# Block-local attention and a squared-gate feed-forward in one kernel: the work from the third unit on in another written order, and pairs of weight pieces in one tile

## The chip, the cores and the metric

The kernel runs on one core of a Trainium2 chip. The metric is the time of the device in microseconds (us), the median of several executions. A profile is taken of one execution; its times count from the first instruction. The engines are named PE (TensorE, matrix products; PEld its weight loads), DVE (VectorE), ACT (ScalarE), POOL (GpSimd) and SP (SyncE, which here only issues DMA transfers). Each engine runs its instructions in the order in which they are written.

## What is computed

Batch 4, 8 heads, 768 positions, 64 columns a head; 3072 tokens of 512 columns go into a feed-forward of 2048 columns.

```python
k_sum = k.reshape(B, H, nb, 32, D).max(axis=3)      # summaries of blocks of 32 keys
v_sum = v.reshape(B, H, nb, 32, D).mean(axis=3)
scores_l = scale * q @ k^T                          # kept where |i - j| < 16
scores_s = scale * q @ k_sum^T + log(32)
a = softmax(concat([scores_l_masked, scores_s]))
x = a @ concat([v, v_sum])                          # heads side by side: 3072 x 512
h = x @ w_in
g = where(h >= 1, h, where(h <= -1, 0, (h + 1)^2 / 4))
out = g @ w_out
```

## The kernel before

The 3072 tokens are cut into seven **units** (0 to 6) of 384, 384, 256 and four times 512 tokens; the first three are the *classic* units. Heads go in four pairs. The feed-forward is cut into 16 blocks f of 128 columns. Each fp32 operand of the feed-forward is split into a rounded high part and a remainder, and a product takes three matmuls (high x low, low x high, high x high).

Units 0 to 2 multiply x by w_in directly (L573). Units 3 to 6 use a scheme with seven products (L598) instead of eight: sums and differences of w_in blocks are prepared once, while units 1 and 2 run, and kept in DRAM (`sets`), eight sets of 14 x 256 columns; in each later unit every set is loaded again in four pieces into a **ring** of rooms, those that held the pieces win 7 to 14 of w_in. The seven x operands lie in the rooms of win 0 to 6.

The weights come in as pieces: 16 of w_in and 16 of w_out, taken two at a time as 16 pairs: (win 0, win 1), then (wout i-1, win i+1), at last (wout 14, wout 15). Each piece is [128, 2, 512] floats and has a room of its own in `wpool`, with a tag such as `win7`. The room takes first some of the first unit's inputs (`FIRST`), then the raw 64-bit words, then the two halves (high and remainder).

The order of all work is written out by hand as two texts, `OPENING` and `REST`. A word is a step: its first sign names a function, the others are hexadecimal numbers (unit, then pair of heads or block or set, then part). Each engine's queue, SP's and POOL's DMA issues too, follows these texts. After `OPENING` two pools are closed, and others are opened in their place: `att_later` (with two rooms of the tag merged), `ps_acc` (4) and `ps_att` (2). The steps that matter here:

| step | what it does | engine, line |
|---|---|---|
| r, k, q, y, v | load raw keys, windowed keys, queries, raw values, windowed values of unit and pair | SP, L294, L305, L321, L326, L339 |
| R, C | maxima of key blocks; their copy behind the windowed keys | DVE L354, POOL L359 |
| s, n, i, g, h, l, t, p | scores; mask; maxima; exponentials; reciprocals; scaling; 12 turns of blocks; values | PE L512, DVE L519, L526, ACT L530, DVE L534, POOL L540, DVE L552, PE L561 |
| u, z, x, X | sums of values, turned, spread; result of attention | DVE, POOL, ACT or DVE |
| F, G, H, I, J, O | product with w_in (unit, block, quarter); gate in three steps; its high part; its remainder | PE L573, ACT L663, L667, DVE L671, ACT L676, POOL L681 |
| B, ( | product with w_out, for all row tiles or for one | PE L694 |
| U, o | result out of the accumulator; its store | ACT L705 or DVE L703, SP L709 |
| %, & | prepare a set; store it in `sets` | POOL, DVE, ACT; SP |
| ^, <, > | differences, high part and remainder of x operands | POOL L486, ACT L494, POOL L498 |
| {cqn | load piece n of set q for unit c into the ring | POOL L585 |
| 1cqn, 9 | product n of set q; its sums | PE L598; DVE L611, ACT L607 |
| a, b, c, d, e | weights: scaling of the top words, low words, joining, high part, remainder | ACT L242, L248, DVE L255, L260, POOL or ACT L267, POOL L272 |

Rooms that are shared: k and v of units 2 and later, the converted words of the weights and, before, the first unit's results are tiles of tag w (3 rooms); r and y of units 2 and later, and v of unit 1, are tiles of tag v (2 rooms); results of unit 1 and later and the tiles of % are tiles of tag merged (2 rooms).

Of the kernel before, what the change touches and what calls it, by code (L numbers as in the profile page):

```python
# [42 lines left out]
CLASSIC = 3  # L43
WIDTH = [sum(n for _, _, n in unit) * QB for unit in BLOCKS]
# [29 lines left out]
F140 F141 t208 v20 t200 F142 &03 y21 t209 %017 H13 I13 t20a J12 O12 x200 t207 t20b F143 t204 t202 F150 t206 J13 t205  # L74
t201 r22 &05 u21 F151 p20 G14 F152 H14 q21 X20 I14 %100 C210 %101 %111 O13 F153 L20 %102 F160 s21 F161 %103 R22 G15
n211 n210 %110 i21 H15 I15 z21 g212 g210 k22 y22 v21 %104 %112 C220 g213 g211 F162 %113 h21 B12 F170 F171 x210 %114
u22 l210 l211 t21b t213 t210 &20 F172 F173 F163 J14 B13 q22 O14 t216 t21a t214 t219 B14 &21 &04 G16 t217 J15 t211 H16
I16 O15 G17 &02 F180 t212 t215 %105 y23 r23 %106 F181 t218 q23 H17 p21 X21 F182 z22 %115 I17 J16 %107 F183 F190 O16
L21 %116 s22 G18 u23 n220 &13 n221 i22 H18 I18 g220 g222 g223 g221 R23 F191 %117 x220 h22 F192 %200 %201 %202 F193 k23
# [15 lines left out]
H27 I27 R41 %612 F290 &62 F291 &63 g320 g325 J27 g321 g326 g322 %613 g324 g323 g327 O26 O27 F292 F293 %614 u40 %615
G29 h32 C330 %701 F283 %700 B26 H29 G28 H28 %702 I29 %703 I28 %704 B27 l320 F2b0 F2b1 %705 J29 J28 %616 l321 F2b2 q33
r42 F2b3 F2a0 F2a1 &30 %706 O28 G2b %617 t325 t323 t32a O29 &65 k40 &70 t320 H2b t326 I2b t321 t329 t32b t328 t327
%707 F2a2 F2a3 B28 J2b G2a H2a <30 O2b {300 F2d0 t324 t322 F2d1 F2d2 F2d3 I2a G2d B29 %711 H2d {303 J2a s33 O2a >30
{302 %710 n330 n331 i33 I2d F2c0 F2c1 F2c2 F2c3 G2c H2c y42 I2c B2a F2f0 v33 F2e0 F2f1 F2e1 F2f2 g335 g331 J2c &71
g336 g330 g333 {311 ^30 %712 F2f3 F2e2 F2e3 B2b {312 g334 &01 g337 %713 g332 %714 R42 h33 O2c C400 G2f u42 l330 l331  # L100
<33 H2f J2d O2d x330 p32 >33 I2f %715 1300 B2c &64 y43 X32 B2d t330 t338 9300 %716 t33b t339 {313 J2f t33a t336 t334
t332 y41 G2e {301 {310 O2f %717 t337 t335 t331 t333 1303 H2e p33 I2e J2e X33 <31 O2e <36 ^31 ^32 s40 <32 B2e u41 n401
n400 B2f i40 <34 >31 g405 g402 g400 >32 1301 9303 1302 k41 &73 >34 G300 g404 g401 g407 ^33 g406 g403 U21 H300 9301
1304 >36 z41 9304 <35 9302 1310 9305 1311 9310 1306 G311 H311 z40 h40 I300 9307 >35 G301 H301 I311 l400 l401 9313 r43
v40 1305 9306 1312 I301 9311 G310 1313 x400 H310 1316 t405 I310 J30 t40b t401 t400 t406 1314 J31 O31 O30 {321 t407 q42
(312 {322 {320 t403 t402 (311 {323 v41 &75 t409 C410 U20 {330 t40a t408 t404 (310 (302 q41 G320 H320 (313 9312 I320
9314 p40 9317 X40 G321 z42 9315 (301 H321 s41 I321 G331 n411 n410 i41 (303 1320 H331 J32 1315 9316 9320 1322 (300 O32
{331 g410 I331 9321 R43 G330 1323 g416 H330 1324 I330 9324 9322 g413 g411 J33 {343 O33 9325 1321 u43 1326 1325 9326
(331 g417 g412 (332 (321 k42 g415 g414 h41 {341 G351 H351 (333 (322 y50 v42 l410 q43 (330 9323 l411 G350 G340 {340
9327 I351 {333 H340 I340 H350 I350 t41b J35 G341 t418 t411 t417 t412 {342 (323 (320 1330 t415 t414 9330 t41a C420 O35  # L110
{332 &72 x410 1331 (350 y52 &74 1332 t419 t413 t410 t416 H341 9331 9333 I341 (351 p41 G360 H360 k50 X41 (353 1340 I360
J34 9340 O34 u50 s42 1342 1333 n420 1334 k43 q50 n421 i42 1335 9332 9334 g425 (343 g421 9335 g420 {351 9336 G371 (341
9341 G370 g424 (352 H370 1344 H371 g426 I370 1336 g427 I371 1343 x420 J37 1341 9342 9337 {350 1345 g423 g422 9344 (342
G361 9345 h42 O37 H361 I361 G391 9346 H391 1346 l421 l420 9343 (340 (372 I391 G390 9347 H390 J36 (370 (373 C430 O36
1350 {353 I390 G380 {363 {352 {361 t420 t424 t42b t42a t423 C500 t422 H380 G381 9350 t428 t429 t421 t425 (363 t427
(362 (371 (361 1352 {360 H381 I380 t426 s43 v43 9351 I381 (360 1353 n431 n430 J39 1355 J38 1354 O39 i43 g436 9354 9352
# [699 lines left out]
```

## Time and profile before

| | |
|---|---|
| runs | 661.37, 664.34, 665.67 us; median 664.34 |
| profiled execution | 661.37 us, its span 659.6 us |
| busy share of the span | PE 94%, PEld 82%, DVE 71%, POOL 65%, ACT 57% |
| mean granted clock of TensorE | 0.977 |
| moved by DMA | 137.27 MB, 208 GB/s over the span |

Busy time of PE is modelled, since matmuls overlap. A row of the timeline has start, duration, engine, line, operation, tiles, count, and in brackets the idle time before it and what ended it. A row of waits has the engine and its instruction, what it waited for, then the total in us, how often, and the longest. A row of a stretch has the busy time of PE, PEld, DVE, ACT and POOL with the number of instructions, the granted clock, the share of the DMA engines and GB/s. A group of instructions has its count, busy us and mean ns of one, and the idle time before it.

### The profile page before, as it was taken

How to read it: one execution, taken by the hardware profiler on the slowest of the kernel's cores; microseconds unless marked ns; L12 is line 12 of the kernel's file. 1: busy time of each engine (PE TensorE's matmuls, PEld its weight loads, DVE VectorE, ACT ScalarE, POOL GpSimd, SP SyncE). 2: the span in 40 equal slices, each digit the busy share in tenths (PEclk: the TensorE clock that was granted, in tenths of full speed). 3: DMA queues.
4: the chain of work that ended last, by engine and by line, in shares of the span. 5: the costliest groups of instructions: out<-in, count | busy, mean ns of one | idle time of the engine just before them, and what ended most of it. 6: DMA issues, size and time to landing. Idle time of an engine off the chain costs nothing.

```text
span 659.6 us, 13521 instructions
## 1 busy us (share of the span) xinstructions
PE 618.7 (94%) x4772; PEld 538.7 (82%) x4772; DVE 466.3 (71%) x1081; ACT 375.8 (57%) x1042; POOL 428.2 (65%) x515
## 2 busy tenths in 40 slices
PE   7789999799999998899989999999989999889896
PEld 7678888678888877778978888888878988779795
DVE  4988786389888899888877978876767774433332
ACT  1789997354645575654557556438445456443343
POOL 1569999555778589855668845579736569542421
PEclk8989999989999999899999999999989999998999
DMA  8969930286776769679699787875668465670631
GB/s 296 309 211 368 299 124 17 95 261 207 221 239 176 230 203 358 155 231 326 204 248 279 203 260 211 258 219 166 177 202 261 133 198 158 188 228 14 209 117 64
DMA packets 90009, 137.27 MB, mean 208 GB/s; under 512 B 27862, under 2 KB 57686, under 8 KB 89942
## 3 DMA queue, kind: packets, MB, share of 16 engines
q1 hardware_dynamic: 71510, 77.68, 39.1%
q0 software_dynamic: 18432, 58.73, 29.0%
q8 instruction: 38, 0.62, 0.4%
q14 instruction: 29, 0.24, 0.1%
HBM read 115.41 MB, written 20.97 MB: 207 GB/s over the span
## 4 chain that ended last, share of the span: by engine, by line
PE 63%; DVE 11%; DMA 11%; ACT 6%; POOL 4%; issue 4%; SPq 0%; DVEq 0%; ACTq 0%; POOLq 0%
PE acc L694 30%; PE h L598 20%; PE h L573 6%; DMA ring<-sets 3%; DVE merged L623 3%; DMA kraw<-in_kT 3%; DMA out<-o 3%; PE s_ps L512 2%; PE o_ps L561 2%; DMA k<-in_kwin 2%; DVE t L671 1%; DVE turned_blocks L552 1%; ACT e L423 1%; POOL glo L681 1%; DMA vraw<-in_vT 1%
## 5 line engine op out<-in xcount | busy, mean ns | idle before, releaser
L694 PE MATMUL acc<-halveswout,ghi 128*128 128x512 f32 x768 | 239.7, 393 | 0.0
L681 POOL TENSOR_TENSOR glo<-t,ghi 128x512 fp32r<-128x512 f32 (+2 forms) x112 | 126.8, 1135 | 115.1 <-ACT ghi L676 102.4
L598 PEld LDWEIGHTS h<-xop,ring 128*128 128x128 f32 x1344 | 176.7, 192 | 25.7 <-DVE t L671 6.5
L598 PE MATMUL h<-xop,ring 128*128 128x256 f32 x1344 | 184.1, 286 | 11.8 <-DMA ring<-sets 4.8
L694 PEld LDWEIGHTS acc<-halveswout,ghi 128*128 128x128 f32 x768 | 145.6, 190 | 25.8
L694 PE MATMUL acc<-halveswout,glo 128*128 128x512 f32 x384 | 154.1, 401 | 2.7 <-ACT o L705 1.7
L663 ACT ACTIVATE t<-h,ones_half 128x256 f32<-128x256 f32 (+1 forms) x176 | 84.2, 489 | 100.7 <-DVE h L611 76.7
L573 PE MATMUL h<-x,halveswin 128*128 128x384 f32 (+1 forms) x576 | 104.8, 329 | 4.7 <-DVE t L671 3.0
L676 ACT CAST ghi<-t 128x512 fp32r<-128x512 f32 (+2 forms) x112 | 62.0, 557 | 72.5 <-PE acc L694 38.3
L552 DVE STREAM_TRANSPOSE turned_blocks<-e 32x256 f32<-32x256 f32 (+1 forms) x240 | 98.3, 409 | 7.0 <-POOL e L540 3.1
L573 PEld LDWEIGHTS h<-x,halveswin 128*128 128x128 f32 x576 | 91.9, 191 | 13.5 <-DVE t L671 5.1
L671 DVE SCALAR_TENSOR_TENSOR t<-h,t 128x256 f32<-128x256 f32 (+1 forms) x176 | 75.2, 442 | 39.1 <-ACT t L667 35.7
L585 POOL DMA_DIRECT2D ring<-sets x128 | 70.7, 558 | 36.0 <-PE h L598 31.0
L694 PEld LDWEIGHTS acc<-halveswout,glo 128*128 128x128 f32 x384 | 73.0, 190 | 16.0 <-ACT o L705 2.1
L667 ACT ACTIVATE t<-t 128x256 f32<-128x256 f32 (+1 forms) x176 | 73.6, 434 | 3.2
L611 DVE TENSOR_TENSOR h<-h,sums_so_far 128x256 f32<-128x256 f32 x128 | 52.2, 427 | 31.9 <-PE h L598 31.1
L611 DVE TENSOR_TENSOR sums_so_far<-h,sums_so_far 128x256 f32<-128x256 f32 x96 | 39.7, 420 | 41.3 <-PE h L598 38.2
L530 ACT ACTIVATE e<-e,den 128x120 f32<-128x120 f32 x144 | 55.1, 384 | 19.1 <-DVE den L526 18.9
L540 POOL TENSOR_TENSOR e<-e,den 128x480 f32<-128x480 f32 (+1 forms) x40 | 35.7, 912 | 20.6 <-DVE den L535 18.7
L623 DVE TENSOR_TENSOR merged<-merged 128x128 f32<-128x128 f32 x64 | 33.2, 528 | 7.0 <-POOL merged L620 5.6
L498 POOL TENSOR_TENSOR xop<-xraw,xop 128x512 fp32r<-128x512 f32 x28 | 36.1, 1300 | 1.8 <-ACT xop L494 1.6
L519 DVE SCALAR_TENSOR_TENSOR e<-s_ps,mask_sb 128x480 f32<-128x480 f32 (+1 forms) x40 | 22.6, 601 | 9.8 <-PE s_ps L512 9.8
(105 smaller groups left out, 660.3 us busy)
## 6 DMA issues: line engine op xcount, KB each, us to landing
ring<-sets POOLq DMA_DIRECT2D x96, 512.0 KB, 5.6
rawwin<-in_w_in SPq DMA_DIRECT2D x16, 512.0 KB, 10.5
rawwout<-in_w_out SPq DMA_DIRECT2D x16, 512.0 KB, 9.7
ring<-sets POOLq DMA_DIRECT2D x32, 256.0 KB, 4.7
out<-o SPq DMA_DIRECT2D x24, 256.0 KB, 5.3
k<-in_kwin SPq DMA_DIRECT2D x12, 480.0 KB, 5.1
v<-in_vwin SPq DMA_DIRECT2D x18, 288.0 KB, 5.7
kraw<-in_kT SPq DMA_DIRECT2D x13, 384.0 KB, 4.7
```

The source lines that it names most:

```text
L530: nc.scalar.activation(out=e, in_=e, func=AF.Exp, bias=dens[c, p][:, 0, u:u + 1], scale=1.0, accum_out=dens[c, p][:, 1, u:u + 1])
L552: nc.vector.transpose(out=turned_blocks[kb * SB:(kb + 1) * SB, :2 * nt, qb * SB:(qb + 1) * SB], in_=e[qb * SB:(qb + 1) * SB, :, at:at + SB])
L573: nc.tensor.matmul(hs[c, f][:, :w], weight["win", f][:, part, k * P:(k + 1) * P], x, start=(k == 0 and n == 0), stop=(k == NK - 1 and n == 2))
L585: nc.gpsimd.dma_start(out=flat, in_=cols)
L598: nc.tensor.matmul(hs[c, q, n][:, :HALF], weights[:, wp, kk], x[:, xp, kk], start=(kk == 0 and m == 0), stop=(kk == 1 and m == 2))
L611: nc.vector.tensor_tensor(out=of if to is None else so_far[:, to], in0=of, in1=so_far[:, so], op=ALU.add)
L663: nc.scalar.activation(out=t, in_=h, func=AF.Relu, bias=ones_half, scale=0.5)
L667: nc.scalar.square(out=t, in_=t)
L671: nc.vector.scalar_tensor_tensor(out=t, in0=h, scalar=1.0, in1=t, op0=ALU.max, op1=ALU.min)
L676: nc.scalar.copy(out=hi, in_=ts[c, f])
L681: nc.gpsimd.tensor_tensor(out=lo, in0=ts[c, f], in1=hi.bitcast(F32), op=ALU.subtract)
L694: nc.tensor.matmul(acc[c, i], a[:, rows], weight["wout", f][:, part], start=(f == first and n == 0), stop=(f == last and n == 2))
```

## The change

1. `REST` is another order of the same 2700 steps and, new in it, the six steps that ended `OPENING` (U00, U01, U02, o02, o01, o00). `OPENING` is otherwise the same.
2. Pairs: both pieces of a pair lie in one tile [128, 2, 2, 512] of tag `w0` to `w15`; pair 14 (`APART`) keeps two tiles, since win 15's room later holds `sums_so_far`. For the 15 others, the scaling of the top words (a), the high part (d) and the remainder (e) are one instruction over 1024 columns where there were two over 512.
3. The x operands and the ring are slices of the pairs' tiles where they were tiles of their own in the same rooms.
4. Of the first unit's results, 0 and 1 now lie in rooms of tag merged; only 2 lies in tag w.

The end of `OPENING` and the beginnings of `REST`:

```diff
-J10 I11 F120 J11 O10 U00 F121 F122 U01 O11 F123 U02 o02 o01 o00
+J10 I11 F120 J11 O10 F121 F122 O11 F123
 REST
-%000 r20 k20 %001 q20 %002 %010 %011 %003 %004 %012 R20 %013 %005 %006 C200 %014 s20 n200 n201 &40 r21 k21 i20 g200
-y20 F130 F131 %015 g203 g201 g202 v22 R21 u20 h20 %007 G12 &00 F132 z20 F133 H12 l201 B10 I12 %016 G13 B11 l200 t203
+k20 F130 U00 r21 q20 r20 U01 R21 R20 C200 G12 U02 H12 F131 F132 F133 s20 I12 G13 H13 n201 n200 o01 %000 %001 o00 i20
+%002 y20 %003 I13 %011 %010 F150 B10 F151 F152 F140 %004 F141 F142 g200 g202 g203 g201 %012 %005 %006 h20 l200 l201
+B11 %013 u20 %014 J12 %007 k21 C210 t201 t205 %015 t202 q21 v20 o02 &31 &60 O12 y21 &40 F153 F143 z20 J13 G14 x200 O13
```

Of the last unit, the ring loads of its sets 2 to 6 with the products that take {631 and its neighbours, other steps left out:

```diff
-{620 {622 {633 {630 {623 {621 {632 {640 {641 {642 {631 1630 1634 1632 {643 {653 {650 {652 {663 {660 {651
+{620 {621 {622 {623 {631 {630 {632 {633 1630 1632 {641 1634 {642 {643 {640 {653 {652 {650 {663 {660 {651
```

The results of unit 5, and the loads of unit 4's first keys between the values of unit 3 and their scores, with the steps of PE there (some F and B ahead of p32 left out):

```diff
-U50 U53 o53 o50 U51 U52 o51 o52
+U50 o50 U51 U53 o51 U52 o53 o52
-k40 s33 v33 p32 1300 B2c B2d 1303 p33 s40
+v33 s33 p32 B2c B2d k40 1300 p33 1310 s40
```

The code, cut:

```diff
+APART = NF - 2
...
+    def room(i, what, shape, dtype):
+        if i == APART:
+            return None, [wpool.tile([P] + shape, dtype, tag=f"{n}{f}", name=f"{what}_{n}{f}") for n, f in pairs[i]]
+        both = wpool.tile([P, 2] + shape, dtype, tag=f"w{i}", name=f"{what}{i}")
+        return both, [both[:, part] for part in range(2)]
...
     def convert_top(i):
-        for _, top in raws[i]:
+        for top in tops[i]:
             nc.scalar.mul(out=top.bitcast(F32), in_=top.bitcast(F32), mul=2.0 ** -112)
...
     def convert_high(i):
-        for part, piece in enumerate(pairs[i]):
-            weight[piece] = room(piece, "halves", [P, 2, DM], F32R)
+        both, parts = room(i, "halves", [2, DM], F32R)
+        weight.update(zip(pairs[i], parts))
+        words = converting[i].bitcast(F32)
+        halves[i] = [(part[:, 0], part[:, 1], words[:, n]) for n, part in enumerate(parts)] if both is None else [(both[:, :, 0], both[:, :, 1], words)]
+        for hi, _, word in halves[i]:
...
-            copy(out=weight[piece][:, 0], in_=converting[i][:, part].bitcast(F32))
+            copy(out=hi, in_=word)
     def convert_rest(i):
...
+        for hi, lo, word in halves[i]:
+            nc.gpsimd.tensor_tensor(out=lo, in0=word, in1=hi.bitcast(F32), op=ALU.subtract)
...
     def x_high(c, n):
-        x_ops[c, n] = wpool.tile([P, 2, 2, HALF], F32R, tag=f"win{n}", name=f"xop{c}_{n}")
+        x_ops[c, n] = weight["win", n].rearrange("p h (b n) -> p h b n", b=2)
...
     def load_set(c, q, n):
-        tag = 7 + 4 * (q % 2) + n
+        at = weight["win", 7 + 4 * (q % 2) + n]
...
-        part = wpool.tile(shape, F32R, tag=f"win{tag}", name=f"ring{c}_{q}_{n}")
...
-        nc.gpsimd.dma_start(out=flat, in_=cols)
+        nc.gpsimd.dma_start(out=at[:, 0] if n == 3 else at.rearrange("p h n -> p (h n)"), in_=cols)
...
     def result(c, i):
-        if c == 0:
+        if (c, i) == (0, NTT - 1):
             o_sb = stage.tile([P, DM], F32, tag="w", name=f"o{c}_{i}", bufs=W_BUFS)
```

More of the change, by code (lines that the diff above doesn't have):

```diff
@@ L75 @@
[L75 to L79, printed above, removed]
@@ L95 @@
[L95 to L99, printed above, removed]
@@ L100 @@
[L100 to L104, printed above, removed]
@@ L165 @@
-9575 G5f1 G5e1 H5e0 H5e1 (5d1 (5d3 H5f0 I5e1 I5e0 I5f0 H5f1 I5f1 >63 {611 >61 (5c1 (5c3 >64 (5c2 <66 (5d0 (5c0 J5f
-1600 1601 O5f {612 ^63 1602 9600 1603 (5f0 (5f3 9601 9603 J5e G600 >66 1604 O5e 9604 9602 (5f1 (5f2 1606 H600 <65 9605
-9607 G601 I600 >65 {613 H601 I601 G611 H611 J60 (5e3 (5e2 1605 (5e0 9606 I611 U50 (5e1 1610 O60 1614 1612 {620 G610
-H610 I610 9610 J61 U53 9611 1613 1611 9613 {622 O61 1616 (611 o53 o50 (613 9612 9614 9615 {633 {630 9617 U51 1615 U52
-G631 G620 G621 H620 9616 G630 I620 (601 {623 H630 H631 H621 I630 I631 I621 (610 (603 (612 (602 1621 (600 {621 1620 J62
@@ new lines @@
+g330 g337 g331 J2c F2f2 F2f3 g333 g332 u41 %703 %712 {312 {303 >30 {301 O2c z40 {310 G2f %704 %713 H2f h33 %705 B2b
+F2e2 <33 %714 z41 I2f %715 l330 l331 F2e3 p32 B2c J2d %706 J2f %716 t330 t335 t333 t336 t338 O2d B2d k40 t33b G2e t331
+t332 %707 %717 O2f >33 {311 t339 t337 t33a t334 r43 &74 &75 H2e X32 I2e 1300 J2e p33 C400 X33 {313 O2e 1310 <31 ^32
+<32 ^31 k41 v41 R42 s40 B2e n401 n400 i40 9300 B2f <34 R43 U21 g406 >31 1301 >32 y43 g404 1302 g402 g405 g403 >34 ^33
+9301 g401 &73 <36 9303 g407 9310 G300 1304 1303 9302 9304 g400 1311 <35 H300 >36 9305 h40 >35 G311 H311 l400 1306 l401
@@ new lines @@
+9575 <64 <63 G5e0 H5e0 G5f1 1575 H5f1 (5d3 (5c3 (5d1 G5e1 <61 >64 >63 I5f1 9576 G5f0 >61 (5c1 (5d0 (5c2 H5e1 H5f0 <66
+I5e0 I5e1 I5f0 (5c0 1604 J5f 1600 1601 9600 {612 {610 O5f 1602 >66 {611 ^63 (5f0 1603 J5e (5f3 <65 O5e {613 >65 (5f1
+9601 (5f2 1606 9602 (5e0 9604 9605 9603 9607 (5e1 (5e2 1605 G611 H611 {620 G600 U50 G601 H601 H600 I611 I601 9606 I600
+1612 (5e3 1610 G610 J60 H610 9610 o50 1614 I610 9611 {621 9612 U51 1611 1613 1615 J61 1616 9614 9616 9613 O60 O61 {622
+9617 U53 G621 o51 9615 G631 H621 (613 (612 G630 (603 (611 (602 H631 I621 I631 H630 G620 U52 H620 I620 1622 {623 1620
@@ L219, in fused_kernel @@
     pairs = [pieces[2 * i:2 * i + 2] for i in range(NF)]
-    weight, raws, converting, joined = {}, {}, {}, {}
-    def room(piece, what, shape, dtype):
-        return wpool.tile(shape, dtype, tag=f"{piece[0]}{piece[1]}", name=f"{what}{piece[0]}{piece[1]}")
+    weight, raws, tops, converting, joined, halves = {}, {}, {}, {}, {}, {}
+    def room(i, what, shape, dtype):
[3 more added lines that the diff above has]
+        return both, [both[:, part] for part in range(2)]
     def fetch(i):
-        raws[i] = []
-        for name, f in pairs[i]:
-            raw = room((name, f), "raw", [P, DM, 2], I32)
+        both, parts = room(i, "raw", [DM, 2], I32)
+        for raw, (name, f) in zip(parts, pairs[i]):
             if name == "win":
@@ L286, in fused_kernel @@
     for i, share in enumerate(FIRST):
-        for piece, (what, p) in zip(pairs[NF - 1 - i], share):
+        _, parts = room(NF - 1 - i, "first", [2 * DM], F32)
+        for flat, (what, p) in zip(parts, share):
             shape = {"q": [NB, P], "k": [NB, KA], "v": [NB, P]}.get(what, [S])
-            flat = room(piece, "first", [P, 2 * DM], F32)[:, :math.prod(shape)]
+            flat = flat[:, :math.prod(shape)]
             at_first[what, p] = flat if len(shape) == 1 else flat.rearrange("p (a b) -> p a b", b=shape[1])
```

194 lines of the change are left out of this document (100 added, 94 removed).

## The prediction, made before the changed kernel was run

> **What bounds the kernel now.** I read the page's first part, then the table of waits of TensorE and of the engines that hold its results, then the timeline around the longest of these waits, and last the stretches of the clock.
>
> ```profile
> span 659.6 us, 13521 instructions
> ...
> PE 618.7 (94%) x4772; PEld 538.7 (82%) x4772; DVE 466.3 (71%) x1081; ACT 375.8 (57%) x1042; POOL 428.2 (65%) x515
> ```
>
> The profiled execution took 661.37 us, 1.8 us beyond its span; the median of the three runs shown is 664.34, so that execution stood 3.0 us below it. TensorE is busy 94%: all that an order can win is the 659.6 - 618.7 = 41 us in which it stands idle, and the time in which it works at a lower clock. So the question is which idle time the new order removes and which it makes.
>
> ```profile
> PE s_ps L512 <- POOL k L359: 5.9, 1, 5.9
> PE h L598 <- DMA ring<-sets: 4.8, 4, 2.4
> ...
> PE acc L694 <- ACT o L705: 1.7, 1, 1.7
> ...
> DVE o L703 <- DMA out<-o: 13.6, 4, 6.4
> ...
> ACT o L705 <- DMA out<-o: 7.6, 2, 6.3
> ...
> PEld h L598 <- DMA ring<-sets: 2.6, 1, 2.6
> ```
>
> Each row has the total, how often, and the longest. One wait of 5.9 us stands out, then 4.8 + 2.6 = 7.4 us for loads of the ring, then 1.7 us for a result that itself waits for an output store.
>
> The long one, in the timeline of all engines:
>
> ```profile
> 97.85 0.33 SPq L339 DMA_DIRECT2D v<-in_vwin  x1
> ...
> 99.74 1.29 POOL L272 TENSOR_TENSOR halveswin<-w,halveswin 128x512 fp32r<-128x512 f32 x1
> ...
> 117.10 0.92 PE L451 MATMUL o_ps<-pt,v 120*64 120x64 f32 x24
> ...
> 124.32 0.69 DVE L703 COPY o<-acc 128x512 f32<-128x512 f32 x1 [1.12 <-PE acc L694]
> ...
> 124.80 2.27 PE L573 MATMUL h<-x,halveswin 128*128 128x384 f32 x12
> ...
> 126.52 1.32 SPq L709 DMA_DIRECT2D out<-o  x3
> 126.62 0.95 POOL L748 MEMSET turned_blocks<- 128x1024 f32 x1
> ...
> 128.02 0.34 SPq L294 DMA_DIRECT2D kraw<-in_kT  x1
> 128.62 0.34 SPq L305 DMA_DIRECT2D k<-in_kwin  x1
> ...
> 131.42 0.95 DVE L354 TENSOR_REDUCE ks<-kraw 128x24 f32<-128x768 f32 x1 [0.26 <-DMA kraw<-in_kT]
> ...
> 132.49 0.40 POOL L359 COPY k<-ks 128x96 f32<-128x96 f32 x1 [2.01 <-DVE ks L354]
> ...
> 132.95 1.08 PE L512 MATMUL s_ps<-k,q 64*64 64x120 f32 x16 [5.88 <-POOL k L359]
> ```
>
> SyncE issues nothing from 97.85 to 126.52: it stands at the three stores of the first unit's results (o02, o01, o00). Behind them in its queue are r20 and k20, the third unit's keys; they go out at 128.02 and 128.62, the raw keys are there 3.4 us later, R20 (DVE) and C200 (POOL) follow, and s20 starts at 132.95.
>
> ```profile
> 60.00:80.00 20.00, 19.61 (x99) 16.97 (x97) 15.74 (x30) 20.00 (x48) 19.29 (x21) 1.00 1.08 330
> ...
> 100.00:120.00 20.00, 19.72 (x145) 17.26 (x144) 10.88 (x23) 13.02 (x33) 16.74 (x18) 1.00 0.01 2
> ...
> 240.00:260.00 20.00, 18.31 (x160) 15.22 (x160) 18.90 (x37) 11.65 (x36) 17.46 (x22) 1.00 0.94 309
> ...
> 133.00:137.60 4.60, 4.60 (x27) 4.30 (x28) 2.57 (x6) 2.51 (x10) 1.27 (x1) 0.50 0.99 276
> 593.80:598.40 4.60, 4.59 (x25) 4.59 (x26) 1.29 (x4) 0.00 (x0) 0.00 (x0) 0.63 0.02 5
> 481.70:485.80 4.10, 4.10 (x17) 3.72 (x18) 1.81 (x5) 1.00 (x6) 0.00 (x0) 0.58 1.14 319
> ```
>
> Columns: stretch, PE, PEld, DVE, ACT, POOL, then granted clock, DMA share, GB/s. The DMA engines are empty (0.01) from 100 to 120. After the long wait TensorE works at clock 0.50 for 4.6 us, which loses 2.3 us; after the two longest ring waits at 0.63 and 0.58, which loses 4.6 x 0.37 = 1.7 and 4.1 x 0.42 = 1.7.
>
> **The change part by part, on the profiled execution.**
>
> *The third unit's loads.* In the new order k20, r21, q20, r20 stand ahead of every store on SyncE. k20's room (a slot of tag w) is free when pair 13 is converted, at about 101 (the row at 99.74); r21 and r20 take the rooms of v12 and v13, the last read by the matmuls at 117.10, so r20 goes out at about 118.1 and is there at 121.5. On DVE, U01 (0.69 from 124.32), R21 and R20 (0.95 each) now stand in a row: R20 is done at 126.9. On POOL the memset at 126.62 and a small one behind it end by about 127.7, C200 (0.40) at 128.1. On PE, F130 to F133 now stand ahead of s20: twelve matmuls of 384 columns, as many as F120 to F123 in the row at 124.80, whose 2.27 us hold about 2.1 of issue. They end at about 129.0, so s20 finds its keys with 0.9 us to spare. The wait goes whole: -5.9, and the clock's loss with it: -2.3. What is late next is C200 and U02, which s20's room waits for as well, 0.8 us behind; so between -6 and -8.3 and I take -8.2. It adds a wait: results 0 and 1 now lie in the two rooms of tag merged, which %000 and %010 need next, so these steps of POOL wait until the stores o01 and o00 have landed.
>
> ```profile
> ring<-sets POOLq DMA_DIRECT2D x96, 512.0 KB, 5.6
> ...
> ring<-sets POOLq DMA_DIRECT2D x32, 256.0 KB, 4.7
> out<-o SPq DMA_DIRECT2D x24, 256.0 KB, 5.3
> k<-in_kwin SPq DMA_DIRECT2D x12, 480.0 KB, 5.1
> ```
>
> %000 thus starts at about 125.4 + 5.3 = 130.7, and POOL stands still from 128.1 on. Behind %000 on POOL are the other % steps, on which only DVE's own % steps and later stores wait, and l200; l200 cannot come before s20, n, i, g and h are through, so 2.6 us there cost nothing; if l200 were ready, they would be paid once. On SyncE, y20 stands behind o01 and o00 and goes out near 127, ahead of the loads' 128.02 of now.
>
> *The ring.* A load costs 5.6 us from issue to landing (4.7 for the small one). I compared how far ahead of its first product each of the 128 loads stands in the order, in TensorE work between the two:
>
> ```profile
> 630.72 2.87 PE h L598 x24
> ...
> 646.22 6.84 PE acc L694 x30
> ```
>
> That is 0.12 us a matmul of 256 columns and 0.228 of 512. In the old order 21 loads stand nearer than they take, short by 34.3 us together; in the new one 13, short by 20.8. POOL mostly runs ahead of TensorE, so only a part is felt: 7.4 us of waits and 3.4 of clock, 10.8 for 34.3. In proportion the new order pays 20.8 / 34.3 x 10.8 = 6.5: -4.3. Bounds: all gone, -10.8; all 20.8 felt with three dips of 1.7, +15. The row that it is nearest to:
>
> ```profile
> 582.28 0.57 POOL L585 DMA_DIRECT2D ring<-sets  x1
> 585.49 0.53 POOL L585 DMA_DIRECT2D ring<-sets  x1 [2.64 <-PE h L598]
> 588.47 1.60 POOL L585 DMA_DIRECT2D ring<-sets  x3 [2.45 <-issue]
> ...
> 593.81 4.54 PE L598 MATMUL h<-xop,ring 128*128 128x256 f32 x24 [2.38 <-DMA ring<-sets]
> ```
>
> {631 goes out second of the three at 588.47, behind {640, {641 and {642, which wait for rooms; the new order has {631 ahead of all {64. That wait and its dip (2.4 + 1.7) should go.
> [...]
>
> *Results.* Unit 5's four results share two rooms. In the old order U50 and U53, then U51 and U52, stand 2.8, 3.6 and 0.7 us of TensorE work apart, in the new one 2.8, 2.9 and 3.4; with 5.3 us a store the fourth now hardly waits. Of the 1.7 us I take -1.0 (0 to -1.7).
>
> *Keys of unit 4.* k40 stands only 2.5 us of TensorE work ahead of s40 (19.2 before) and takes 5.1: up to +2.6, and a dip of 1.7. v33, now written ahead of it, holds one of the three rooms of tag w, so k40 waits for p32 to give back another; that is two B steps, 2.7 us, ahead of its place in the order, so SyncE may send it earlier. Hence +1.0 (0 to +4.3).
>
> *Pairs in one tile.* Fifteen of 16 pairs are scaled, copied and subtracted in one instruction where there were two.
>
> ```profile
> L681 POOL TENSOR_TENSOR glo<-t,ghi 128x512 fp32r<-128x512 f32 x64 | 82.3, 1289 | 93.8 <-ACT ghi L676 81.7 <-issue 11.8
> ...
> L676 ACT CAST ghi<-t 128x512 fp32r<-128x512 f32 x64 | 39.3, 619 | 49.5 <-PE acc L694 27.5 <-DVE t L671 21.5
> ...
> L681 POOL TENSOR_TENSOR glo<-t,ghi 128x384 fp32r<-128x384 f32 x32 | 32.6, 1022 | 16.9 <-ACT ghi L676 16.8
> ...
> L676 ACT CAST ghi<-t 128x384 fp32r<-128x384 f32 x32 | 16.2, 509 | 13.8 <-PE acc L694 10.8 <-DVE t L671 2.9
> ```
>
> POOL: 1289 - 1022 = 267 ns a 128 columns, so 221 ns of an instruction do not depend on its size; ACT: 110 and 179. Saved: POOL 22 x 0.22 = 4.8 us, ACT 23 x 0.18 = 4.1 us. From 60 to 80 both are full (20.00 and 19.29 of 20), but so is PE (19.61). I take -1.0; bounds -3 (the few starts where PE waits for a converted weight) and +0.7 (the scaling of a pair now waits for both loads, and everything behind it on ACT). The slices x_ops and the ring move no instruction: 0, between -1 and +2 if a room's reader now counts for its neighbour.
>
> *What is late next.* The rest of the order is shuffled by small distances: every s and p stands within 4.5 us of TensorE work of its old place. But DVE is busy 18.90 of 20 from 240 to 260, and TensorE will ask for the same DVE work in less time. I take back +2.0 (0 to +6).
>
> Sum: -8.2 - 4.3 - 1.0 + 1.0 - 1.0 + 2.0 = -11.5: 661.4 to 649.9; put on the median, 664.3 - 11.5 = 652.8, **653**.
>
> **The rivals.**
>
> 1. *Only the start pays.* Other waits appear in place of the ring's, of the same sum: -8.2 + 2.0 = -6.2, **658**. For it: a ring load is late by POOL's place in its queue, which any order has somewhere. Against: 13 short loads for 21.
> 2. *Slower: loads written nearer than they take.* k40, {420 (2.1 us ahead, behind O41 on POOL), {343 (1.4) and {330 (4.1) stand close. If POOL and SyncE reach these only at their place in the order, the whole shortfall is felt: 20.8 + 2.6 + four dips of 1.7 = 30.2 where 10.8 were, so 664.3 - 8.2 + 19.4 - 2.0 + 2.0 = **675.5**. It makes the kernel slower from the point at which 19 of the 30.2 us are felt, 0.63, against 10.8 of 34.3, 0.31, now.
> 3. *The change does not do what it says*: the new loads are still held, by r20's room, by R20 behind U01, or by s20's room behind U02, and s20 starts near 132 as before. Then the rest alone, -3.3: **661**. Against: the 0.9 us to spare above; but it is small beside 5.9.
> **How the numbers follow.** Chances: forecast 0.57, rival 1 0.21, rival 2 0.10, rival 3 0.12. About 1% (6.6 us) is what a measurement of this kernel can tell from no change: faster is below 657.7, slower above 671. Faster: nearly all of the forecast (0.54) and half of rival 1 (0.10): 0.64. Slower: rival 2, 0.10. The rest, 0.26, is the same. The forecast's own bounds reach from 644 (ring waits all gone, -6.5; opening at its end, -2) to 659 (DVE taking back 6 for 2, k40 at 3). With rivals 1 and 3 inside, the range is 644 to 664.
>
> **What would show it.** Right: no wait of s_ps for POOL k above 1 us near 130, kraw issued before 120, the clock at full between 120 and 140; fewer or shorter waits of h L598 for the ring, none behind {631; two or fewer dips after 250. Wrong: SyncE idle again up to 126; a new wait of s_ps at unit 4 for k; POOL standing before %000 for longer than 3 us with DVE or ACT behind it; ring waits over 10 us; DVE's share above 95% between 140 and 260 with p waiting for turned_blocks.

## The result, and the profile after

The changed kernel takes 639.99 us (median of four runs, 638.79 to 641.18) where the kernel before, beside it, takes 664.14: a ratio of 0.964, 95% interval 0.960 to 0.968. That is 24 us; 11.5 were forecast, and 640 lies below the range of 644 to 664. The profiled execution took 640.93 us, 20.4 less than that of before; the other 3.7 us come of where the two stood, before's 2.8 below its median and after's 0.9 above. One of the five runs of f_s33, told below, was slowed as a whole (677.75 us at a mean clock of 0.845) and is left out there.

The first part of the page, and the waits of the engines (engine, line and releaser: total us, how often, the longest):

```profile
span 638.8 us, 13478 instructions
...
PE 612.0 (96%) x4772; PEld 535.7 (84%) x4772; DVE 459.7 (72%) x1081; ACT 372.7 (58%) x1019; POOL 425.2 (67%) x493
```

```profile
DVE o L708 <- DMA out<-o: 7.1, 2, 6.4
...
DVE ks L361 <- DMA kraw<-in_kT: 5.1, 1, 5.1
...
PE h L603 <- DVE sums_so_far L616: 4.2, 1, 4.2
```

In the changed code the lines are numbered 4 to 7 higher, and the ring and the x operands are slices of tiles called halves. The 5.9 us of s_ps for k have left the list of TensorE's waits, and the ring's 7.4 have shrunk to one of 1.1 ("PE h L603 <- DMA halves<-sets"). A new wait leads among those behind 125 us: 4.2 us for sums_so_far, which VectorE writes, and VectorE itself stood 5.1 us for raw keys.

Windows of the page before and after do not lie over the same work. So I cut TensorE's order into stretches and took for each the *lost time*: the distances between the starts of successive matmuls, less the distance that the same shape has when nothing holds it (0.119 us for 256 columns, 0.230 for 512, and so on; 580.2 us in all in every kernel). Slow clock counts as loss too. The first column gives each stretch's place in the trace of before; us lost in one execution each; the two right columns are experiments told below.

```
stretch of before         before  after   after-before  forecast | p_late  f_s23
opening, to 125            25.1    25.2      +0.1         -1.0   |  25.0    25.2
third unit's start -157     9.8     1.0      -8.8         -8.2   |  11.2     1.0
units 2 and 3     157-247   7.3     5.5      -1.8          -     |   7.2     8.2
hand-over         247-298  10.6     7.1      -3.5         +1.0   |   9.5    10.9
raw keys r50      298-350   3.4     2.6      -0.8          -     |   3.0     9.2
raw keys r52      350-404   2.5     7.8      +5.3          -     |   8.2     2.3
                  404-475   1.4     2.2      +0.8          -     |   1.2     1.6
ring {521         475-500   4.3     0.9      -3.4      \         |   0.4     3.0
                  500-570   1.0     0.9      -0.1       | ring   |   0.9     1.0
unit 5's results  570-582   2.0     0.0      -2.0  -1.0 | -4.3   |   0.0     3.7
ring {631         582-608   4.3     0.0      -4.3      /         |   0.0     4.4
ring {65, end     608-654   2.1    -0.1      -2.2                |  -0.1     1.1
sum                        73.8    53.1     -20.7        -11.5   |  66.6    71.5
```

The forecast also took back +2.0 for VectorE, with no place. Kernels with the same order in a stretch agree there within 1 us in most stretches, but the opening moves by 3 and a stretch with a wait by 1 to 6, which one column cannot show. At r50 it hides a gain: the eight executions with before's order there lost 3.2 to 9.2 us, the eight with the new order 1.9 to 3.0.

### The profile page after: what moved, and what is told of

Its sections match the earlier page's. It is cut to its first block, busy times and chain, and to the rows that moved or that the text cites. A ratio compares the mean times of both kernels' runs of the same rounds, so it can differ in the third digit from the quotient of the medians.

```text
span 638.8 us, 13478 instructions
## 1 busy us (share of the span) xinstructions
PE 612.0 (96%) x4772; PEld 535.7 (84%) x4772; DVE 459.7 (72%) x1081; ACT 372.7 (58%) x1019; POOL 425.2 (67%) x493
## 4 chain that ended last, share of the span: by engine, by line
PE 55%; DVE 8%; DMA 3%; POOL 3%; ACT 1%; issue 1%; DVEq 0%; POOLq 0%
PE acc L699 27%; PE h L603 22%; DVE turned_blocks L559 3%; PE o_ps L568 2%; PE s_ps L519 2%; PE h L580 2%; DMA kraw<-in_kT 2%; DVE merged L628 1%; DMA halves<-sets 1%; POOL halves L505 1%; DVE t L676 1%; ACT e L537 1%; POOL xraw L493 1%; DVE e L526 1%; DVE sums_so_far L616 1%
## 5 line engine op out<-in xcount | busy, mean ns | idle before, releaser
L699 PE MATMUL acc<-halves,ghi 128*128 128x512 f32 x720 | 224.2, 393 | 0.0
L603 PEld LDWEIGHTS h<-halves,halves 128*128 128x128 f32 x1344 | 176.3, 192 | 18.4 <-DVE sums_so_far L616 4.9
L603 PE MATMUL h<-halves,halves 128*128 128x256 f32 x1344 | 183.3, 286 | 6.4 <-DVE sums_so_far L616 4.2
L699 PEld LDWEIGHTS acc<-halves,ghi 128*128 128x128 f32 x720 | 136.0, 189 | 24.2
L699 PE MATMUL acc<-halves,glo 128*128 128x512 f32 x360 | 143.8, 399 | 0.7 <-POOL glo L686 0.7
L676 DVE SCALAR_TENSOR_TENSOR t<-h,t 128x256 f32<-128x256 f32 (+1 forms) x176 | 74.7, 443 | 36.3 <-ACT t L672 35.0
L580 PE MATMUL h<-x,halves 128*128 128x384 f32 (+1 forms) x540 | 95.9, 324 | 4.1 <-POOL halves L278 2.5
L580 PEld LDWEIGHTS h<-x,halves 128*128 128x128 f32 x540 | 85.3, 189 | 10.8 <-POOL halves L278 3.6
L589 POOL DMA_DIRECT2D halves<-sets x128 | 70.7, 557 | 29.5 <-PE h L603 26.2
L699 PEld LDWEIGHTS acc<-halves,glo 128*128 128x128 f32 x360 | 68.2, 189 | 12.9 <-issue 1.9
L278 POOL TENSOR_TENSOR halves<-w,halves 128x1024 fp32r<-128x1024 f32 x15 | 36.1, 2411 | 5.4 <-ACT halves L274 4.8
## 6 DMA issues: line engine op xcount, KB each, us to landing
raw<-in_w_in SPq DMA_DIRECT2D x15, 512.0 KB, 10.6
```

Source lines behind the costliest of these rows:

```text
L580: nc.tensor.matmul(hs[c, f][:, :w], weight["win", f][:, part, k * P:(k + 1) * P], x, start=(k == 0 and n == 0), stop=(k == NK - 1 and n == 2))
L589: nc.gpsimd.dma_start(out=at[:, 0] if n == 3 else at.rearrange("p h n -> p (h n)"), in_=cols)
L603: nc.tensor.matmul(hs[c, q, n][:, :HALF], weights[:, wp, kk], x[:, xp, kk], start=(kk == 0 and m == 0), stop=(kk == 1 and m == 2))
L676: nc.vector.scalar_tensor_tensor(out=t, in0=h, scalar=1.0, in1=t, op0=ALU.max, op1=ALU.min)
L699: nc.tensor.matmul(acc[c, i], a[:, rows], weight["wout", f][:, part], start=(f == first and n == 0), stop=(f == last and n == 2))
```

## The experiments

**Halves of the order.** A step already done is skipped, so a kernel can follow one order up to a step and then the other for all that is left:

```diff
- REST = <order of before>
+ REST = <order of the changed kernel up to X> + <order of before, without what is done>
```

The first changed over right behind o00.

> The kernel before with one part of the new order: from the second unit on it begins as the changed kernel does (third unit's raw keys, keys and queries asked for first, U00 and U01 behind the first R20, s20 early, the new rule for the first unit's result tiles), up to the store o00; from there on everything stands as before, and every piece of weight keeps its own tile. Theory 1, each wait belongs to its own place: only the stretch around 130 us changes, by 7.9 to 8.7 us in the two traces, so 664.1 - 8.4 = 655.7 (654 to 658), the clock is full from 120 to 140, and the waits at 263, 452, 482, 530 and 594 us of before are found again, each 8 us earlier. Theory 2, the head start is handed on (loads, DVE and ring get ahead of TensorE): the waits at the hand-over to the seven-product units and the ring's go too, 650 or less.

Measured: 659.06 us, ratio 0.9965 (0.993 to 1.000), so neither theory's time. Up to the place that is at 146 us in the trace of before it won 8.0 us, as the changed kernel did; right behind that place, at 138 us of its own trace, 4.1 us and a slow clock were lost:

```profile
142.42 2.29 PE L573 MATMUL h<-x,halveswin 128*128 128x384 f32 x6 [4.13 <-DVE t L671]
```

```profile
DVE sums L369 <- DMA vraw<-in_vT: 2.5, 1, 2.5
```

The gate's step t on VectorE was queued behind u20, and u20 waited for the raw values y20, sent at 131.8 and there at 137.8. The changed order has y20 earlier; the hybrid had it in the old place. I changed over later.

> The changed kernel with its own order up to s23 (unit 2's last scores, 168 us) and from there the order of before. The first hybrid, which changed over right behind o00, won 8.0 us at 130 us and lost 5.7 again at 138 us, where VectorE stood behind raw values asked for late; this one changes over later. Theory 1, each wait belongs to its own place: 8.8 us won up to 143 us, the rest of the waits of before found again (hand-over to unit 3 near 255, the ring near 445, 475, 585 us): 664.1 - 8.8 = 655.3, a ratio of 0.987. Theory 2, the head start is handed on to the loads behind: the hand-over's 4.0 us go too, 651 or less, 0.981 or less. Theory 3, before's order cannot hold a head start, since its later loads and VectorE work are written for a later start: new waits give it back, 0.993 or more.

> The changed kernel with its own order up to s33 (unit 3's last scores, 234 us), from there the order of before. Theory 1: 8.8 + 1.0 us won up to there, and before's order at the hand-over to the seven-product units (k40, s40, the first ring and x operands) keeps its 4 us of waits and its dip: 664.1 - 9.8 = 654.3, ratio 0.985. Theory 2, the hand-over's waits come of VectorE's work being late (18.90 of 20 busy), which the order up to s33 has already moved ahead: 650, 0.979.

> The mirror of it, in the changed kernel's code: the order of before up to s33, from there the order of the changed kernel. Theory 1, the later gains are the later order's own: hand-over -3 to -4, 290 to 330 us -2.4, the new wait for raw keys +7, then -3.7, -2.0, -4.2, -2.2 near the places where before's ring and out stores were late: 664.1 - 12 = 652 or so without the start, ratio 0.982 (0.977 to 0.986). Theory 2, they need the start's 8 us: 658 or more, 0.991 or more.

> The order of before up to 1322 (about 290 us) and the changed kernel's from there, three steps apart at the change-over. Theory 1, the later gains and the later loss are that order's own: the new wait for raw keys of about +7 near 390 us, and the ring's and the out store's waits gone (-2.4 near 345, -1 near 390, -3.7 near 482, -2.0 near 577, -4.2 near 595, -2.2 near 620): 664.1 - 8 = 656, ratio 0.988, and no wait of h for the ring above 0.5 us after 300 us. Theory 2, the ring's waits go because TensorE comes earlier or later to them than before, through the start: some of the ring's waits remain, 660 or more.

> The order of before up to %514 (about 217 us) and again from 1322 on (about 290 us); between them, over the hand-over to the seven-product units, the order of the changed kernel; in the changed kernel's code. Only five steps stand on the other side of the first change-over and three of the second. Theory 1, the hand-over's gain is that stretch's own order (VectorE's work and the x operands spread earlier), whatever came before: -4 to -5 there, the dip at 264 us gone, 664.1 - 4.5 = 659.6, ratio 0.993. Theory 2, it is the start's head start: no change there, ratio 0.998 or more.

| kernel | order of the changed kernel | us | ratio to before, 95% |
|---|---|---|---|
| f_s23 | up to s23 | 654.19 | 0.986 (0.983 to 0.989) |
| f_s33 | up to s33 | 657.52 | 0.993 (0.991 to 0.996) |
| g_s33 | from s33 on | 659.08 | 0.995 (0.994 to 0.997) |
| p_late | from 1322 on | 652.57 | 0.984 (0.981 to 0.988) |
| m_hand | from %514 to 1322 | 663.21 | 1.001 (0.998 to 1.004) |

f_s23 is theory 1's number: the new order up to s23 is worth 8 us by itself, and behind it before's waits are found again. The column above is of its slowest run (659.41 us), which lost 9.2 at r50: there VectorE stood 5.2 us for raw keys and TensorE 4.2. p_late shows the other half: without the start, from 350 us on every stretch of its column is after's within 1.0 us, the new loss of raw keys among them (8.2). The one wait of the ring that it has, 1.5, is more than I had allowed:

```profile
PE h L603 <- DVE sums_so_far L616: 4.4, 1, 4.4
PE h L603 <- DMA halves<-sets: 1.5, 1, 1.5
```

So the late gains need no head start. The two halves multiply to 0.986 x 0.984 = 0.970, 644 us; the other 4 lie between them, in units 2 and 3 and the hand-over, where the hybrids fail as a test. By their times g_s33 and m_hand fit their theory 2, and f_s33 fits neither of its theories. But g_s33 and m_hand made waits of their own at the change-over (g_s33 lost 17.0 in the hand-over for before's 10.6, since u42 stood 6.3 us on VectorE for raw values: "DVE sums L376 <- DMA vraw<-in_vT: 8.0, 2, 6.3"; m_hand lost 10.3 in units 2 and 3 for 7.3). In the hand-over itself m_hand's profiled execution lost 7.8, as the changed kernel does (7.1 to 8.1): in this one execution the gain there goes with the stretch's own order, and what was lost ahead of it hides it in the time. Of f_s33 only the times are read; why it won less than f_s23 stays open.

**Order and tiles apart.** c_order is the code of before with the changed order; b_pairs the changed code with the order of before.

> The code of before, each piece of weight in its own tile, with the order of the changed kernel and its rule for the first unit's result tiles. Theory 1, all of the gain is the order's: 640.0 (638 to 643), with the wait for the raw keys of unit 5 near 373 us as in the changed kernel. Rival, the room of a pair is what lets the loads of the ring and of the third unit go early: 650 or more, with waits for the ring behind {421, {521 or {631.

> The code of the changed kernel with the order of before, and the first unit's result tiles as before: only a pair of weight pieces in one tile, and rooms as slices of it. Theory 1: the time that the two traces have in common up to 126 us shows that the fewer ACT and POOL instructions are worth nothing to TensorE: 664.1, between 662 and 666. Prediction on record: -1.0, 663. Rival: the slices make a load or a product wait for its neighbour, or free it from one: 667 or more, or 658 or less.

b_pairs: 662.79 us, 1.001 (0.997 to 1.004); the pairs are worth nothing that can be measured, and the stretch up to 125 us loses the same. The engines did work less, POOL 2.9 us (428.2 before) and ACT 1.8 (375.8):

```profile
PE 615.7 (93%) x4772; PEld 536.0 (81%) x4772; DVE 465.7 (71%) x1081; ACT 374.0 (57%) x1019; POOL 425.3 (64%) x493
```

c_order: 643.34, 0.968 (0.963 to 0.974), just above theory 1's range; its interval holds the changed kernel's 0.964. What its profiled execution lacks lies at the raw keys r52, where VectorE stood 7.6 us instead of 5.1 ("DVE ks L354 <- DMA kraw<-in_kT: 7.6, 1, 7.6") and 10.6 were lost for 7.8.

**The ring and the result store.** Four steps of before moved:

```diff
- O62 9621 O63 {640 ... {641 ... {642 {631
+ O62 9621 O63 {631 {640 ... {641 ... {642
- U50 (5e1 1610 O60 ... o53 o50        + U50 (5e1 1610 O60 o50 ... o53
- O66 {653 o52 G680 {650 {652          + {652 9641 ... {650 O66 {653 o52 G680
```

> The kernel before with four steps moved in units 5 and 6: the ring load {631 ahead of {640 (it stood behind {640 {641 {642), {652 ahead of 9641 and {650 ahead of O66 (both stood behind O66 and o52), and the store o50 behind O60, ahead of o53. Theory 1, the place in POOL's and SyncE's queue is all there is to these waits: at 594 us the 2.4 us wait and the slow clock behind it go (-4.2), at 614 to 618 us two waits (-2.2), at 574 us the wait of acc for a result tile (-2.0): 664.1 - 8.4 = 655.7, ratio 0.987. Rival: the loads that are moved past come late instead ({640, {653): 0.993 or more.

655.49 us, 0.9915 (0.988 to 0.995). At {631 the loss went from 4.3 to 0.1, as expected; at the result store 2.0 to 0.9; at {652 and {650 from 2.1 to 1.3:

```profile
PE h L598 <- DMA ring<-sets: 1.1, 1, 1.1
PE acc L694 <- ACT o L705: 0.6, 1, 0.6
```

That is 6 us, and the time lies between the two expected (0.987 and 0.993). At r50, which it did not touch, this execution lost 2.9 more than before's. The loads moved past did not come late, {640 landing 13.4 us ahead of its use and {653 5.9, so the rival's reason is refuted; the wait of 1.1 is for {651, which had not been moved and took 7.1 us. Then the contrary: in the changed kernel {631, which stands 8.4 us of TensorE work ahead of its product, put 2.1 ahead of it, nearer than in the kernel before (3.5):

```diff
- (600 (601 1624 {631 1623 ...           + ... I640 (623 {631 (630 1630 ... 1632
```

> The changed kernel with one ring load, {631, written late: just ahead of (630, 2.5 us of TensorE work ahead of the product 1632 that reads it, where its transfer takes 4.5 to 5 us; {630, {632 and {633 stand ahead of it, {641 and {642 behind. Theory 1, a load's written distance decides (the rule of the prediction): 1632 waits some 2.5 us and the clock drops behind it, +2.5 to +4 near 575 us. Theory 2, what decides is whether something ahead of it in POOL's queue is itself waiting for TensorE: nothing is, POOL sends it near 569 or 570 us, 5 us or more ahead of its use, and the loss is 0 to 0.5.

640.12 us, 0.965 (0.962 to 0.967), the changed kernel's time. POOL's timeline (start, length, what):

```profile
567.27 1.31 POOL L686 TENSOR_TENSOR glo<-t,ghi 128x512 fp32r<-128x512 f32 x1
568.51 1.10 POOL L589 DMA_DIRECT2D halves<-sets  x2
570.59 0.53 POOL L589 DMA_DIRECT2D halves<-sets  x1 [0.98 <-PE h L603]
```

The second of the two at 568.51 is {631, at 569.07. It landed at 573.74 and was used at 574.96: 5.9 us ahead for a written distance of 2.1. Theory 2 holds, and the rule of the prediction falls for this load. The whole list points the same way. With each load's own transfer time, 21 loads of before stand nearer than they take, short by 45.6 us, and 15 of after, by 28.6; POOL sends them far earlier than written:

```
          written ahead   sent ahead   took
{330 after     4.1           13.2       5.0
{343 after     1.4            7.4       3.1
{630 after     4.8           14.2       7.6
{621 before    1.4            9.6       8.8
{521 before    4.5            8.7       8.6   late
{631 before    3.5            4.8       4.8   late
```

{631 was late in the kernel before since the loads ahead of it in POOL's queue were waiting for TensorE to leave their rooms; i_late, which moved it ahead of them, shows it. {521 is another case: it was sent 8.7 us ahead, and its transfer took 8.6. In the changed kernel it was sent 8.1 ahead and took 5.9. No run isolates what made that transfer shorter.

**The new wait.** The timeline of the changed kernel:

```profile
363.29 0.91 SPq L312 DMA_DIRECT2D k<-in_kwin  x2
364.29 0.43 SPq L301 DMA_DIRECT2D kraw<-in_kT  x1
...
369.15 0.68 DVE L708 COPY o<-acc 128x512 f32<-128x512 f32 x1
...
374.96 0.95 DVE L361 TENSOR_REDUCE ks<-kraw 128x24 f32<-128x768 f32 x1 [5.12 <-DMA kraw<-in_kT]
...
377.97 2.93 PE L603 MATMUL h<-halves,halves 128*128 128x256 f32 x12 [4.24 <-DVE sums_so_far L616]
```

The raw keys r52 go out at 364.29, behind k52, and land 10.6 us later. VectorE reaches R52 at 369.8, 5.5 us after they went out (a load of the median 5.2 us would have been there), and stands; the sums that TensorE needs are queued behind it, and TensorE stands 4.2 us. The first mend asks for r52 earlier and reaches R52 later:

```diff
- {420 k52 {433 ... g511 r52 1420 ... C520 R52 u53 ... t514 C521
+ {420 r52 k52 {433 ... g511 1420 ... t514 C520 R52 u53 C521
```

> The changed kernel with two places in its order mended: the raw keys r52 of unit 5 are asked for ahead of the keys k52, and C520, R52 and u53 stand just ahead of C521 (some 5 us of TensorE work later). Theory 1: VectorE stood 5.05 us behind R52, which waited for those raw keys, and TensorE's 4.4 us of waits for sums_so_far at 373 us and the 6.8 us at half clock behind them were its price: 7.0 of loss goes, 640.0 - 6.5 = 633.5 (632 to 636). Rival: the transfers are the limit at that place (DMA busy 0.90 from 360 to 380), and the wait moves to the ring, to k52 or to s52: 637 to 641.

640.09 us, 0.964 (0.959 to 0.969): by its times no better than the changed kernel, though its profiled execution took 637.06. That is the rival's number, but not by a queue that it named. VectorE no longer waits for the keys; of the 7.8 us lost in that stretch 5.2 stayed (2.5 in before), since another queue now waits:

```profile
POOL k L366 <- DVE ks L361: 4.4, 1, 4.4
...
PE acc L699 <- POOL glo L686: 2.7, 1, 2.7
```

POOL stood at C521 for R52, which now stood behind nine transposes (4.0 us) on VectorE, and behind C521 stood the remainder of a gate. The second mend leaves C520 and puts R52 and u53 ahead of those transposes. In TensorE's work R52 then stands 7.0 us later than in the changed kernel, not 3 as I wrote.

> The changed kernel unaltered, to stand beside the mended one in the same rounds: 640 (638 to 641), ratio 0.964, with 7 us of loss near 373 us where VectorE waits some 5 us for the raw keys r52.

> The changed kernel with r52 asked for ahead of k52, as in the first mend, but with R52 and u53 only some 3 us of TensorE work later, ahead of the block transposes t510 instead of behind them, and C520 left where it was. In the first mend 3.6 us of the 7.0 were left, since POOL stood 4.4 us at C521 behind R52 behind nine transposes, and the rest of a gate behind POOL. Theory 1: the raw keys land about 2.4 us earlier and R52 is reached about 3 us later, so that neither VectorE nor POOL waits more than 1 us: 6 of the 7.0 us go, 633 to 635, ratio to before 0.956, faster than the changed kernel by 0.8 to 1%. Rival: the transposes of unit 5, now 2 us later, become the wait (values p51 for turned_blocks): 637 to 639.

Measured side by side, the changed kernel took 640.67 us (638.03 to 642.79; 0.966, 0.963 to 0.969) and the mended one **636.16** (635.18 to 637.38; 0.959, 0.957 to 0.962): every run of the one is below every run of the other. The medians differ by 4.5 us, 0.7%, somewhat under what I expected; the stretch lost 3.6 where the changed kernel beside it lost 8.0. From 360 to 380 us of the mended kernel, its clock (third from the right) is full and TensorE works 18.80 us where the changed kernel has 15.76 and 0.91; what TensorE still waits for is there too:

```profile
360.00:380.00 20.00, 15.76 (x146) 13.76 (x145) 12.90 (x31) 10.33 (x32) 8.51 (x13) 0.91 0.90 284
```

```profile
360.00:380.00 20.00, 18.80 (x168) 16.50 (x167) 14.74 (x37) 11.53 (x35) 11.23 (x17) 1.00 0.93 288
```

```profile
PE o_ps L568 <- DVE turned_blocks L559: 1.3, 1, 1.3
PE h L603 <- DMA halves<-sets: 1.2, 1, 1.2
```

Part of the rival's wait came, then: 1.3 us for transposes. Which of the two moves pays is not shown: asked for at 362.10, ahead of k52, the keys landed at 370.29, 4.6 us earlier than in the changed kernel and 0.5 after the time at which that kernel's VectorE reached R52. The earlier request alone may do most of it.

**The hand-over.** Two attempts at one cause. n_dve takes R42 and u42 off VectorE's queue ahead of the transposes that p33 needs; q_s40 puts s40 behind B2e.

```diff
- R42 h33 ... u42 ... t333 1303 ... p33       + h33 ... t333 R42 u42 y43 y41 1303 ... p33
- p33 ... s40 <32 B2e                          + p33 ... <32 B2e s40
```

> The kernel before with four steps moved at the hand-over: R42 and u42 (2.2 us of VectorE's work for unit 4) stand behind t333, the last block transpose of unit 3, instead of ahead of the transposes, and the raw values y43 and y41, which wait for their rooms, follow behind them. Theory 1: VectorE's queue is the bound there, 10 us of work in a row from 252 to 262 us ahead of the turned blocks that p33 needs; the waits of 1.05 us ahead of 1300 and 1.59 us ahead of p33, and the clock's dip behind them at 264 us, go for the most part: -2.5 to -4 in the stretch from 250 to 270 us, ratio 0.995. Rival: the waits there come of something else (k40, the x operands on POOL), or the same 2.2 us are asked for a little later: 0 +- 1 in that stretch.

> The kernel before with one step moved: the scores s40 stand behind B2e instead of ahead of it, so that TensorE has some 2 us of work between p33 and s40, as the changed kernel has between these two (the product 1310). Theory 1: the 1.3 us of waits at s40 (0.66 for VectorE's copy xraw of p33's bank, 0.36 and 0.3 behind it) and the 1.7 us of the clock's dip from 264 us come of s40 standing directly behind p33: -1.5 to -3 in the stretch from 255 to 270 us, ratio 0.996. Rival: B2e itself has to wait for the gate's rest on POOL, or the later s40 makes p40 late: 0 to +1.

n_dve: 666.58 us, 1.006 (1.003 to 1.008), slower by 0.6%. The transposes began when they had before, the first row being before's and the second n_dve's:

```profile
256.69 5.38 DVE L552 STREAM_TRANSPOSE turned_blocks<-e 32x256 f32<-32x256 f32 x12
```

```profile
256.84 5.38 DVE L552 STREAM_TRANSPOSE turned_blocks<-e 32x256 f32<-32x256 f32 x12
```

They wait for POOL's scaling (L540), which ended at 256.62 and at 256.77, and not for VectorE's queue, and y41, moved back, made u41 stand 4.5 us. Theory 1 is false. q_s40: 662.68, 1.001 (0.998 to 1.004); the waits at s40 went, B2e waited 0.8 instead, and the stretch lost 10.0. Its rival holds. In the stretch the losses of more than 0.25 us at one matmul sum to 7.7 in before, at ten places, and to 4.9 in after, at eight; which of them the order removed first stays open.

## Why the prediction was wrong

The direction was right and five terms were not. By the table the sum missed by 9.2 us: 5.6 at the ring, 4.5 at the hand-over and some smaller ones, less 3.3 by which the new wait went beyond what the forecast took back. The 3.7 us between profiles and medians come on top. None of these alone carries 652.8 out of the range. Point by point:

- *Third unit's loads*, -8.2: right, -8.8, and step by step. The timeline of after:

```profile
118.17 0.33 SPq L301 DMA_DIRECT2D kraw<-in_kT  x1
...
125.04 1.80 DVE L361 TENSOR_REDUCE ks<-kraw 128x24 f32<-128x768 f32 x2
...
125.28 1.19 SPq L714 DMA_DIRECT2D out<-o  x2
...
126.57 0.41 SPq L333 DMA_DIRECT2D vraw<-in_vT  x1
...
127.77 0.26 POOL L366 COPY k<-ks 128x96 f32<-128x96 f32 x1
128.00 2.81 POOL L625 TENSOR_TENSOR merged<-halves 128x256 f32<-128x256 f32 x4
...
129.20 0.64 PE L519 MATMUL s_ps<-k,q 64*64 64x120 f32 x16
```

  r20 at 118.17 (118.1 forecast), both sums done at 126.84 (126.9), C200 at 127.77 to 128.03 (128.1), y20 at 126.57 (127), s20 at 129.20 (129.0). Only %000 was not as forecast: it began at 128.00, straight behind C200, and not at 130.7, so the stores sent at 125.28 did not hold it; that changes no term. The clock is full from 120 to 140:

```profile
120.00:140.00 20.00, 20.00 (x114) 17.76 (x113) 13.53 (x38) 10.78 (x26) 12.15 (x18) 1.00 0.66 214
```

- *The ring*, -4.3: the largest miss. The three ring stretches give -3.4 - 4.3 - 2.2 = -9.9. The failed step is "in proportion the new order pays 20.8 / 34.3 x 10.8 = 6.5": it pays 1.1. A load's written distance says little about its lateness as long as POOL is ahead of TensorE, and j_631 shows a load written 2.1 us ahead, with a transfer of 4.7, that costs nothing. Late was {631, held behind loads that themselves waited for TensorE (shown by i_late), and {521, whose transfer took 8.6 us (its -3.4 was not isolated). The prediction had the mechanism for {631, named its price (4.1, measured 4.3), and then went back to the proportion for the sum. Its bound "all gone, -10.8" was close to the answer.
- *Results*, -1.0: -2.0, the whole of the wait. A mis-sized term; i_late shows o50's place to be half of it.
- *Keys of unit 4*, +1.0: no such wait. The stretch gained 3.5 in these two executions and about 2 by most others (before's order loses 9.4 to 10 there where the clock does not drop, after's 7.1 to 8.1). m_hand's profiled execution has the gain with that stretch's order alone; which step of it pays is not isolated.
- *Pairs*, -1.0: nothing (b_pairs). The engines' saving was over-estimated too: 4.8 and 4.1 us were forecast for POOL and ACT, 2.9 and 1.8 came, and TensorE did not wait for them there.
- *What is late next*, +2.0 for VectorE between 240 and 260: wrong in kind and in place. The same work lies some 11 us earlier in after. VectorE was as busy there, 18.77 of 20 us, and TensorE worked more, 19.49 where it had 18.31:

```profile
229.00:249.00 20.00, 19.49 (x172) 16.93 (x170) 18.77 (x49) 12.65 (x38) 18.84 (x25) 1.00 0.89 274
```

  The new wait came at 373 us, +5.3 in its stretch, with VectorE idle and not busy. A term for it could have been had, though not its size. In TensorE's work r52 stands 2.8 us ahead of R52 in the changed order (36.3 before) and r50 30.3 (0.0 before), while a load of raw keys takes 5 us at the median; that r52 would take twice as long was not on record. The trace of before shows the price at r50: VectorE stood 2.7 us, TensorE 1.7 behind it.

```profile
DVE ks L354 <- DMA kraw<-in_kT: 2.7, 1, 2.7
...
PE h L598 <- DVE t L671: 1.7, 1, 1.7
```

  I had measured the distances of k, s, p and the ring, and not those of the loads that VectorE waits for.

The rivals: 1 (only the start pays) is refuted by p_late; 2 (loads nearer than they take) is refuted by its time, 675.5, and by the loads that it named: k40, {420 and {330 cost nothing; a load of its kind did cost, r52, which it had not named; 3 is refuted by the rows above. The signs set out beforehand came as "right" would have them, none as "wrong"; none of them looked at the loads that VectorE waits for.

## What to carry to other kernels

In a hand-written order, price a load by the queue in front of which its reader waits: an engine that is off the bound and stands at a missing transfer holds everything behind it, and that is what the bounding engine feels. Written distance between a load and its use matters most where the issuing engine cannot run ahead, that is, where something in front of the load waits for the bounding engine itself; and where the DMA engines are busy, a transfer takes longer than its median (8.6 us for {521, 10.6 for r52). Compare two orders by those two lists (reader's queue, issuer's queue) before adding up anything in proportion, and look in the old profile for the rows that already show the price, however small. As a forecast this is only partly tried: by it i_late was to win 8.4 us, and it won about 6.

## What the runs showed of the hardware

The granted clock changes in steps of 3.413 us: every stretch of half clock in the table is one, two or three of them. Gaps of TensorE of 1.4 us and more behind 125 us, from sixteen profiled executions (before, after, and all kernels above but f_s33):

```
gap us       gaps   followed or met by a half clock   length of it, us
1.4 to 2.0    26        8                             3.4 (one pair of gaps: 6.8)
2.0 to 2.9    13       10                             3.4
4.1 to 6.0    10       10                             6.8
6.0 to 7.8     7        7                             6.8 or 10.2
```

So a gap of 2.1 us can cost 1.7 more (before, 482 us) and one of 2.75 nothing (first mend, 381 us). The Trainium skill, page "TensorE: Matmul & The Clock Gate", Part 1, has a window of about 3.4 us that runs freely, and the step's length agrees. The same part of the Trainium skill's page gives as its abstract rule that TensorE should have no idle gaps above about 3.4 us; here that is not enough, since 18 of the 39 gaps below 2.9 us met a slow window too.

The same traces show what decided. Lay windows of one step on each execution's own steps, behind 125 us, and take those at full clock: all 27 in which TensorE was idle for 1.92 us or more (by the modelled ends of its matmuls) were followed by half clock, 9 of the 12 with 1.65 to 1.92 us, and none of the 2344 with less. About half a window of idle time, in one gap or in several, is thus the price here. The gap of 2.75 us in the first mend fell into two windows, 1.91 us in one and 0.84 in the next. The steps lie elsewhere in each execution (the long dip of the changed kernel begins at 376.6 us in one and at 375.7 in another), so a clock loss behind a single gap between some 1.7 and 3.8 us is a matter of where the gap falls, and should stand in a sum as a chance.

A load of raw keys took 10 to 13 us in the busy stretch near 370 (364.3 to 374.9; in c_order 365.1 to 378.2), against a median of 5.2 on the page. In the two mended kernels the same load, sent 2.2 and 2.5 us earlier and ahead of k52, took 8.2 and 7.5.
